# Loading and turning the first pair's q and k: strips of 128 bytes and VectorE transposes, or whole rows and fp32 products

## The chip, the cores and the metric

The kernel runs on one core of a Trainium2 chip. The metric is the device time of one execution in microseconds (us). Three runs of the kernel before took 267.16, 268.35 and 268.5 us, median 268.35; the run of 267.16 us is the profiled one. Its span, from the first to the last instruction, is 265.2 us, so 1.96 us lie around the span.

## The reference, cut to what matters

Attention over chunks of keys, followed by a mixture-of-experts layer with one expert per token. For each query the 24 chunks of 32 keys are ranked by an upper bound on their scores, made from the minimum and maximum of the chunk's keys in each dimension; only the best 6 chunks take part in the softmax.

```python
B, H, S, D = 4, 8, 768, 64          # attention; chunk = 32, top_k = 6
k_min, k_max = np.min(k_chunks, axis=3), np.max(k_chunks, axis=3)
ub = np.sum(np.maximum(q * k_min, q * k_max), axis=-1)   # broadcast over query x chunk
ub = np.where(causal, ub, -1e9)
top_chunks = np.argsort(ub, axis=-1)[..., -top_k:]
scores = np.where(sel & causal_by_token, (q @ k.T) / 8, -1e9)
attn = softmax(scores) @ v
x = attn.transpose(0, 2, 1, 3).reshape(B * S, H * D)     # 3072 x 512
# then: argmax expert per token, at most 80 tokens kept per expert (those with the largest gate),
# out[token] = gate * (relu(x @ w1[e]) @ w2[e]),  8 experts, 512 -> 1024 -> 512
```

## The kernel before, in words

The 32 (batch, head) combinations are worked in 16 pairs of heads: pair i holds heads 2p and 2p+1 of batch b, one in partitions 0 to 63 and the other in 64 to 127 (partition = head dimension, free axis = 768 tokens). The code is written out by hand in the order of issue; each engine works through its own instructions in that order, and a helper (`op`) adds the semaphore waits that follow from the names of what is read and written. So the order on an engine is the order in the source.

For each pair, q and k are needed turned: `qT` and `kT`, 64 dimensions by 768 tokens for both heads. In the kernel before, `load` brings q and k with four DMAs each (L377): a DMA of group g takes head g // 2, half g % 2 of the 64 dimensions, in pieces of 32 fp32 numbers (128 bytes), 768 pieces per DMA, so placed that VectorE's transpose of 32 x 32 blocks (`take_q` L456, `take_k` L466) leaves the tokens in order. For the first pair SP issues the groups of head 0 and ScalarE's queue those of head 1, k before q, and the loads of pair 1 and of v follow on SP. Then VectorE takes the minimum (`kmm`, L468) and the maximum (`kmx`, L471) of each chunk and their difference (L473), and ScalarE makes `rq`, the positive part of q (`take_r`, L460): the bound of a chunk is q . min + relu(q) . (max - min).

`bounds` (L489) forms that in PSUM with 16 products: eight on `qT` with the minima, then eight on `rq` with the differences. `score_mm` (L584) follows: q k products for the first steps into the PSUM tiles `SC0`, `SC1` and half of `OB`. Meanwhile `bounds_out` on VectorE turns the bounds, takes the eight largest of each query (L503) and marks the chunks that are not selected (`uns`, L508). `unselT` turns these marks by products (L520) and ScalarE copies them out (`unsT`, L525); products with `ind` (L606), a constant that spreads a chunk over its 32 keys, add the mask to the scores. ScalarE takes the exponentials (`EXB`, L616), GpSimd and VectorE clear the diagonal and add up the sums, and `values` (L731) multiplies by v. From there the loop over the pairs runs, with the bounds of the next pair made while the current one is finished. A gather of the selected tokens and the experts' products follow at the end.

`ind` is made once: VectorE fills it, GpSimd cuts the steps into 32 partitions of each half (L423, L425), and two ScalarE copies (L428) double them into the other 32.

`warm(n, w)` (L1178) issues n products of the bf16 identity with w columns into `SC0`. Nothing reads them; they keep TensorE busy. In the kernel before 52 products of 152 columns stand ahead of everything else on TensorE, and the first pair is then taken with

```python
warm(52, 152)
take_k(0, 0)      # VectorE: transpose k, minimum
take_q(0)         # VectorE: transpose q
take_r(0)         # ScalarE: relu(q)
take_k(0, 1)      # VectorE: maximum, difference
bounds(0)
```

Of the kernel before, what the change touches and what calls it, by code (L numbers as in the profile page):

```python
# [4 lines left out]
ALU = mybir.AluOpType  # L5
ACTF = mybir.ActivationFunctionType
# [4 lines left out]
AX = mybir.AxisListType.X  # L11
# [3 lines left out]
CHUNK = 32  # L15
# [132 lines left out]
def bass_quest_chunk_select__then__topk_capacity_drop_kernel(  # L148
# [10 lines left out]
    B, H, S, D = q.shape  # L159
# [4 lines left out]
    NT = S // 128  # L164
    NCH = S // CHUNK
# [42 lines left out]
    with ExitStack() as pers:  # L208
# [8 lines left out]
        ident_f = al(pers, "ident_f", [128, 128])  # L217
        ident_bf = al(pers, "ident_bf", [128, 128], BF16)
# [4 lines left out]
        sy = Sync(nc)  # L223
        op = sy.op

        with nc.Block(no_gpsimd_drain=True) as blk:

            @blk.sync
            def _body(_unused):
                sp = nc.sync  # L230
                gp = nc.gpsimd
                ve = nc.vector
                ac = nc.scalar
                pe = nc.tensor


                SC = [al(pers, f"SC{i}", [128, 1024], F32, True) for i in range(2)]
                OB = al(pers, "OB", [128, 1024], F32, True)
# [5 lines left out]
                qn = [al(pers, "qn", [128, NT, 2, D]) for _ in range(NB)]  # L244
# [3 lines left out]
                qT = [al(pers, "qT", [128, S]) for _ in range(2)]  # L248
# [118 lines left out]
                def load(i, what="qkv", eng="sp", gs=range(4), hs=(0, 1)):  # L367
                    b, p, s = i // NPB, i % NPB, i % NB
                    base = (b * H + 2 * p) * S * D
                    for nm, src, dst in (("qn", q, qn), ("kn", k, kn), ("vn", v, vn)):  # L370
                        if nm[0] not in what:
                            continue
                        if nm != "vn":
                            for g in gs:
                                a = bass.AP(src.tensor, src.offset + base + (g // 2) * S * D + (g % 2) * 32, [[D, 32], [32 * D, NCH], [1, 32]])
                                o = bass.AP(dst[s], g * 32 * 2 * NT * D, [[2 * NT * D, 32], [32, NCH], [1, 32]])
                                op(eng, lambda: sy.queue[eng].dma_start(o, a), w=[f"{nm}{s}{g}"], dsem=f"d_{nm}{s}{g}")  # L377
                            continue
                        for h in hs:
                            a = bass.AP(src.tensor, src.offset + base + h * S * D, [[D, 128], [128 * D, NT], [1, D]])  # L380
                            o = dst[s][:, :, h, :]
                            op(eng, lambda: sy.queue[eng].dma_start(o, a), w=[f"{nm}{s}{h}"], dsem=f"d_{nm}{s}{h}")
# [38 lines left out]
                for h in range(2):  # L421
# [2 lines left out]
                                                      base=0, channel_multiplier=-CHUNK), r=["ind"], w=[f"ind{h}"])  # L424
                    op("gp", lambda: gp.affine_select(o, o, pattern=[[-1, S]], compare_op=ALU.is_ge, fill=0.0,  # L425
                                                      base=CHUNK - 1, channel_multiplier=CHUNK), r=[f"ind{h}"], w=[f"ind{h}"])
                for h in range(2):
                    op("act", lambda: ac.activation(ind[h * 64 + 32:h * 64 + 64, :], ind[0:32, :], ACTF.Copy), r=["ind", "ind0"], w=[f"ind{h + 2}"])  # L428
                WG = ["wg0", "wg1"]

                def wload(e, part, after=()):
# [22 lines left out]
                def take_q(i):  # L454
                    j, s = i % 2, i % NB
                    op("dve", lambda: ve.transpose(qT[j][:], qn[s][:].rearrange("p a b c -> p (a b c)")),  # L456
                       r=[f"qn{s}{g}" for g in range(4)], w=[f"qT{j}"])

                def take_r(i):
                    op("act", lambda: ac.activation(rq[:], qT[i % 2][:], ACTF.Relu), r=[f"qT{i % 2}"], w=["rq"])  # L460

                def take_k(i, part=None):
                    j, s = i % 2, i % NB
                    kv = bass.AP(kT[j], 0, [[S, 128], [CHUNK, NCH], [1, CHUNK]])
                    if part != 1:
                        op("dve", lambda: ve.transpose(kT[j][:], kn[s][:].rearrange("p a b c -> p (a b c)")),  # L466
                           r=[f"kn{s}{g}" for g in range(4)], w=[f"kT{j}"])
                        op("dve", lambda: ve.tensor_reduce(kmm[j][:, 0, 0:NCH], kv, AX, ALU.min), r=[f"kT{j}"], w=[f"kmm{j}"])  # L468
                    if part == 0:
                        return  # L470
                    op("dve", lambda: ve.tensor_reduce(kmx[:], kv, AX, ALU.max), r=[f"kT{j}"], w=["kmx"])  # L471
                    e, q = ("gp", gp) if i > 1 else ("dve", ve)
                    op(e, lambda: q.tensor_tensor(kmm[j][:, 1, 0:NCH], kmx[:], kmm[j][:, 0, 0:NCH], ALU.subtract),  # L473
                       r=[f"kmm{j}", "kmx", "ind0", "ind1"], w=[f"kmd{j}"])

                def stripes(t, off, row, lo, n):

# [697 lines left out]

                def warm(n, w):
                    for _ in range(n):
                        op("pe", lambda: pe.matmul(SC[0][:, 0:w], ident_bf[:], bass.AP(ident_bf, 0, [[128, 128], [0, 2], [1, w // 2]]), start=True, stop=True),  # L1178
                           r=["ident_bf"], w=["SC0"], inc=False)

                def keep_warm(n, o=SC[0], k="SC0"):
# [7 lines left out]
                        op("pe", lambda: pe.matmul(M0[pr, 0:65], ident_f[:, pr], ident_f[:, 0:65], start=True, stop=True),  # L1189
                           r=["ident_f"], w=["M0"], inc=False)  # L1190

                warm(52, 152)
                take_k(0, 0)
                take_q(0)
                take_r(0)
                take_k(0, 1)
                bounds(0)
                score_mm(0, 0)
                score_mm(0, 1)
# [369 lines left out]
```

## Time and profile before

| | |
|---|---|
| median of 3 runs | 268.35 us (267.16 to 268.5) |
| profiled execution, its own time | 267.16 us |
| its span | 265.2 us |
| TensorE products (PE) | 253.8 us busy, 96% of the span |
| VectorE (DVE) | 211.3 us, 80% |
| GpSimd (POOL) | 206.5 us, 78% |
| ScalarE (ACT) | 160.9 us, 61% |
| DMA | 48.38 MB, 148619 packets, 131583 of them under 512 bytes |

The busy share of TensorE counts the `warm` products, which compute nothing. What sets the end is read from the chain that the profiler follows back from the last instruction; in the first 9 us this chain does not run over TensorE, though that engine is shown busy for most of them.

### The profile page before, as it was taken

To read this page: it belongs to the slowest core of one execution; us is meant where nothing else is said; L and a number is where in the kernel's file an instruction comes from. 1 tells how busy PE (TensorE), PEld (TensorE's weight loads), DVE (VectorE), ACT (ScalarE), POOL (GpSimd) and SP (SyncE) were. 2 spreads that over 40 slices of the span, in tenths; PEclk is the share of its full clock that TensorE was granted. 3 is DMA by queue.
4 is the path that set the end of the run, shared out by engine and by line. 5 is a ranking of instruction groups with operands and counts; after the bars stand their busy time and mean duration, and the time that the engine had idled before them with its cause. 6 is when DMAs were issued, how large, how long until landed. Compare 5 with 4: busy or idle time off the path is not lost.

```text
span 265.2 us, 9859 instructions
## 1 busy us (share of the span) xinstructions
PE 253.8 (96%) x4160; PEld 167.2 (63%) x4160; DVE 211.3 (80%) x592; ACT 160.9 (61%) x260; POOL 206.5 (78%) x288
## 2 busy tenths in 40 slices
PE   7799999999999999999999999999999999888993
PEld 7367576767666666666665656666556557665662
DVE  6887687687989988859899889899999988953342
ACT  3386757575787665656785656565865676841220
POOL 5168869895999798979998989988999942725842
PEclk9999999999999999999999999999999999999999
DMA  9989998999999989999999999969999982912771
GB/s 147 179 142 167 140 308 179 296 214 221 166 209 196 221 131 211 193 220 138 201 207 217 171 161 189 213 123 298 292 241 213 231 189 23 188 45 48 155 149 65
DMA packets 148619, 48.38 MB, mean 182 GB/s; under 512 B 131583, under 2 KB 138870, under 8 KB 148512
## 3 DMA queue, kind: packets, MB, share of 16 engines
q1 hardware_dynamic: 113552, 23.23, 44.9%
q0 software_dynamic: 9936, 18.64, 37.8%
q10 hardware_dynamic: 25088, 5.90, 11.3%
q8 instruction: 32, 0.52, 0.8%
q14 instruction: 11, 0.09, 0.1%
HBM read 57.03 MB, written 11.01 MB: 257 GB/s over the span
## 4 chain that ended last, share of the span: by engine, by line
PE 87%; DMA 4%; ACT 4%; DVE 2%; issue 1%; ACTq 1%; POOL 0%; DVEq 0%
PE OB L731 27%; PE SC L584 19%; PE SC L572 7%; PE SC L606 6%; PE MM L489 4%; PE OB L1499 4%; PE SC L1473 4%; PE MM L772 4%; PE MM L744 3%; DMA qn<-x_rows,idx 3%; PE OB L820 2%; DMA qn<-in_q_dram 2%; ACT EXB L616 1%; PE OB L572 1%; PE MM L811 1%; PE MM L529 1%
## 5 line engine op out<-in xcount | busy, mean ns | idle before, releaser
L616 ACT ACTIVATE EXB<-SC 128x1024 f32<-128x1024 f32 (+2 forms) x87 | 81.2, 947 | 33.3 <-PE SC L584 16.3
L684 POOL TENSOR_TENSOR ES<-ES,EXB 128x512 f32<-128x512 f32 (+1 forms) x73 | 77.6, 1066 | 4.9
L731 PE MATMUL OB<-EXB,vn 128*64 128x256 f32 (+2 forms) x640 | 69.3, 364 | 0.0
L584 PE MATMUL SC<-qT,kT 64*128 64x256 f32 (+3 forms) x376 | 60.8, 435 | 0.3
L731 PEld LDWEIGHTS OB<-EXB,vn 128*64 128x64 f32 x640 | 42.2, 137 | 21.0 <-issue 8.3
L684 POOL TENSOR_TENSOR ES<-EXB 128x512 f32<-128x512 f32 (+1 forms) x29 | 45.3, 1563 | 1.8
L584 PEld LDWEIGHTS SC<-qT,kT 64*128 64x128 f32 x376 | 31.1, 187 | 12.1 <-issue 7.7
L606 PE MATMUL SC<-unsT,ind 64*128 64x320 bf16 (+9 forms) x286 | 34.9, 303 | 0.1
L668 POOL TENSOR_SCALAR_AFFINE_SELECT EXB<-EXB 128x256 f32<-128x256 f32 x63 | 28.9, 465 | 5.0 <-ACT EXB L616 5.0
L739 ACT ACTIVATE oT<-OB 128x512 f32<-128x512 f32 (+1 forms) x32 | 15.7, 490 | 24.4 <-PE OB L731 24.4
L668 POOL TENSOR_SCALAR_AFFINE_SELECT ES<-EXB 128x256 f32<-128x256 f32 x15 | 6.3, 419 | 20.5 <-PE MM L772 13.7
L572 PE MATMUL SC<-qT,kT 64*64 64x256 f32 (+5 forms) x256 | 21.7, 436 | 0.0
L606 PEld LDWEIGHTS SC<-unsT,ind 64*128 64x128 bf16 (+1 forms) x286 | 12.3, 100 | 14.1 <-issue 7.4
L456 DVE STREAM_TRANSPOSE qT<-qn 128x768 f32<-128x768 f32 x16 | 15.5, 971 | 5.4 <-PE SC L606 4.9
L460 ACT ACTIVATE rq<-qT 128x768 f32<-128x768 f32 x16 | 13.5, 845 | 6.0 <-DVE qT L456 5.7
L534 ACT ACTIVATE unsT<-MM,cb 128x384 bf16<-128x384 bf16 (+1 forms) x30 | 14.2, 525 | 4.2 <-PE MM L529 4.0
L466 DVE STREAM_TRANSPOSE kT<-kn 128x768 f32<-128x768 f32 x16 | 15.5, 968 | 1.0 <-DMA kn<-in_k_dram 1.0
L468 DVE TENSOR_REDUCE kmm<-kT 128x24 f32<-128x768 f32 x16 | 15.3, 953 | 0.5
L471 DVE TENSOR_REDUCE kmx<-kT 128x24 f32<-128x768 f32 x16 | 15.1, 941 | 0.0
L503 DVE MAX8 top<-MM 128x8 f32<-128x8 f32 (+4 forms) x160 | 14.6, 166 | 0.6
L753 DVE STREAM_TRANSPOSE MM<-MM 128x192 f32<-128x192 f32 x16 | 6.3, 393 | 9.5 <-PE MM L772 9.2
L847 DVE TENSOR_TENSOR xp<-OB,rden 128x768 bf16<-128x768 f32 x14 | 13.4, 954 | 0.4
(274 smaller groups left out, 456.5 us busy)
## 6 DMA issues: line engine op xcount, KB each, us to landing
w1s<-in_moe_w_dram POOLq DMA_DIRECT2D x8, 1024.0 KB, 10.3
w2s<-in_moe_w_dram POOLq DMA_DIRECT2D x7, 1024.0 KB, 14.9
kn<-in_k_dram SPq DMA_DIRECT2D x62, 96.0 KB, 3.7
qn<-in_q_dram SPq DMA_DIRECT2D x62, 96.0 KB, 3.9
vn<-in_v_dram ACTq DMA_DIRECT2D x28, 192.0 KB, 5.7
out_dram<-w1s SPq DMA_DIRECT2D x2, 1536.0 KB, 6.7
out_dram<-out_dram SPq DMA_DIRECT2D x2, 1536.0 KB, 9.4
x_rows<-xp SPq DMA_DIRECT2D x7, 384.0 KB, 4.6
```

The costliest lines, as they stand in the source:

```text
L456: op("dve", lambda: ve.transpose(qT[j][:], qn[s][:].rearrange("p a b c -> p (a b c)")), r=[f"qn{s}{g}" for g in range(4)], w=[f"qT{j}"])
L466: op("dve", lambda: ve.transpose(kT[j][:], kn[s][:].rearrange("p a b c -> p (a b c)")), r=[f"kn{s}{g}" for g in range(4)], w=[f"kT{j}"])
L468: op("dve", lambda: ve.tensor_reduce(kmm[j][:, 0, 0:NCH], kv, AX, ALU.min), r=[f"kT{j}"], w=[f"kmm{j}"])
L471: op("dve", lambda: ve.tensor_reduce(kmx[:], kv, AX, ALU.max), r=[f"kT{j}"], w=["kmx"])
L572: op("pe", lambda: pe.matmul(o, kT[j][pr, k0:k0 + 64], qT[j][pr, q0 + cut:q1], start=not flags, stop=bool(flags)), r=[f"kT{j}", f"qT{j}"], ...
L584: op("pe", lambda: pe.matmul(o, kT[j][pr, ts(kt)], qT[j][pr, x0:x1], start=not flags and (not cols or cols[0] == 0) and n == 0, stop=bool( ...
L606: op("pe", lambda: pe.matmul(ps[ot, h * 512 + c0 + x:h * 512 + c1], ind[pr, k0:k0 + (64 if halves else 128)], unsT[j][pr, b0 - 128 + x:q1 ...
L616: op("act", lambda: ac.activation(Ex(st, None, 0, W, turned(i)), src, ACTF.Exp, scale=SCALE), r=pk, w=[f"E{st}"])
L668: op("gp", lambda: gp.affine_select(ad, a, pattern=[[0, 2], [1, 128]], compare_op=ALU.is_ge, fill=0.0, base=0, channel_multiplier=-1), r=[ ...
L684: op(e, lambda: sy.queue[e].tensor_tensor(o, in0, in1, ALU.add), r=[f"E{s2}", f"E{first[0]}"] if first else [f"E{s2}"] + (["E5"] if (s2, c ...
L731: op("pe", lambda: pe.matmul(OB[pr, q0:q1], vs[:, kt - RT, h, :] if kt >= RT and turned(i) else vn[s][:, kt, h, :], ex, start=(n == 0), st ...
L739: op("act", lambda: ac.activation(oT[:, q0:q1], OB[:, q0:q1], ACTF.Copy), r=[f"O{bk}"], w=[f"oT{bk}"])
```

## The change

For the first pair alone (i == 0) q and k are loaded in whole rows. A head comes with two DMAs: in the first each of the 128 partitions receives four consecutive tokens (1024 bytes), 512 tokens in all, in the second two consecutive tokens (512 bytes), the other 256. Both queues issue as many DMAs as before, in the same order.

The two VectorE transposes of this pair are gone. `turn_first` turns by products: one of six tiles of 64 dimensions by 128 tokens is the stationary operand and the fp32 identity the moving one, 6 tiles x 2 heads for k into `OB` and as many for q into `SC1`. The tokens of a tile are 4 (or 2) apart, so a product writes every fourth (or second) fp32 number of the PSUM row, and together the products leave the tokens in order. Minimum and maximum are taken from PSUM; ScalarE copies `qT`, `rq` and, last, `kT` out of PSUM. The two copies of `ind` move behind these three on ScalarE. The `warm` products become 6 of 456 columns ahead of the k products, 1 of 152 between k and q, and 4 of 456 behind q. The difference for pair 0 no longer waits for `ind`; for pair 1 it still names it.

```diff
--- before.py
+++ after.py
@@ -372,6 +372,12 @@
                             continue
                         if nm != "vn":
                             for g in gs:
+                                if i == 0:
+                                    n, t0 = (4, 0) if g % 2 == 0 else (2, 4)
+                                    a = bass.AP(src.tensor, src.offset + base + g // 2 * S * D + t0 * 128 * D, [[n * D, 128], [1, n * D]])
+                                    o = bass.AP(dst[s], g // 2 * NT * D + t0 * D, [[2 * NT * D, 128], [1, n * D]])
+                                    op(eng, lambda: sy.queue[eng].dma_start(o, a), w=[f"{nm}{s}{g}"], dsem=f"d_{nm}{s}{g}")
+                                    continue
                                 a = bass.AP(src.tensor, src.offset + base + (g // 2) * S * D + (g % 2) * 32, [[D, 32], [32 * D, NCH], [1, 32]])
                                 o = bass.AP(dst[s], g * 32 * 2 * NT * D, [[2 * NT * D, 32], [32, NCH], [1, 32]])
                                 op(eng, lambda: sy.queue[eng].dma_start(o, a), w=[f"{nm}{s}{g}"], dsem=f"d_{nm}{s}{g}")
@@ -424,8 +430,6 @@
                                                       base=0, channel_multiplier=-CHUNK), r=["ind"], w=[f"ind{h}"])
                     op("gp", lambda: gp.affine_select(o, o, pattern=[[-1, S]], compare_op=ALU.is_ge, fill=0.0,
                                                       base=CHUNK - 1, channel_multiplier=CHUNK), r=[f"ind{h}"], w=[f"ind{h}"])
-                for h in range(2):
-                    op("act", lambda: ac.activation(ind[h * 64 + 32:h * 64 + 64, :], ind[0:32, :], ACTF.Copy), r=["ind", "ind0"], w=[f"ind{h + 2}"])
                 WG = ["wg0", "wg1"]
 
                 def wload(e, part, after=()):
@@ -471,7 +475,7 @@
                     op("dve", lambda: ve.tensor_reduce(kmx[:], kv, AX, ALU.max), r=[f"kT{j}"], w=["kmx"])
                     e, q = ("gp", gp) if i > 1 else ("dve", ve)
                     op(e, lambda: q.tensor_tensor(kmm[j][:, 1, 0:NCH], kmx[:], kmm[j][:, 0, 0:NCH], ALU.subtract),
-                       r=[f"kmm{j}", "kmx", "ind0", "ind1"], w=[f"kmd{j}"])
+                       r=[f"kmm{j}", "kmx"] + (["ind0", "ind1"] if i else []), w=[f"kmd{j}"])
 
                 def stripes(t, off, row, lo, n):
 
@@ -1175,7 +1179,7 @@
 
                 def warm(n, w):
                     for _ in range(n):
-                        op("pe", lambda: pe.matmul(SC[0][:, 0:w], ident_bf[:], bass.AP(ident_bf, 0, [[128, 128], [0, 2], [1, w // 2]]), start=True, stop=True),
+                        op("pe", lambda: pe.matmul(SC[0][:, 0:w], ident_bf[:], bass.AP(ident_bf, 0, [[128, 128], [0, 4], [1, w // 4]]), start=True, stop=True),
                            r=["ident_bf"], w=["SC0"], inc=False)
 
                 def keep_warm(n, o=SC[0], k="SC0"):
@@ -1189,11 +1193,29 @@
                         op("pe", lambda: pe.matmul(M0[pr, 0:65], ident_f[:, pr], ident_f[:, 0:65], start=True, stop=True),
                            r=["ident_f"], w=["M0"], inc=False)
 
-                warm(52, 152)
-                take_k(0, 0)
-                take_q(0)
-                take_r(0)
-                take_k(0, 1)
+                def turn_first(n, ps, keys):
+                    for t in range(NT):
+                        lo, w = (t, 4) if t < 4 else (512 + t - 4, 2)
+                        for h in range(2):
+                            src = bass.AP(n, h * NT * D + t * D, [[2 * NT * D, 128], [1, D]])
+                            op("pe", lambda: pe.matmul(bass.AP(ps, h * 64 * 1024 + lo, [[1024, 64], [w, 128]]), src, ident_f[:], start=True, stop=True),
+                               r=[f"{'k' if n is kn[0] else 'q'}n0{2 * h + (t > 3)}", "ident_f"], w=keys, inc=(t == NT - 1 and h == 1))
+
+                kf = OB[:, 0:S].rearrange("p (c k) -> p c k", k=CHUNK)
+                warm(6, 456)
+                turn_first(kn[0], OB, ["O0", "O1"])
+                op("dve", lambda: ve.tensor_reduce(kmm[0][:, 0, 0:NCH], kf, AX, ALU.min), r=["O0", "O1", "kmm0"], w=["kmm0"])
+                warm(1, 152)
+                turn_first(qn[0], SC[1], ["SC1"])
+                op("act", lambda: ac.activation(qT[0][:], SC[1][:, 0:S], ACTF.Copy), r=["SC1"], w=["qT0"])
+                op("act", lambda: ac.activation(rq[:], SC[1][:, 0:S], ACTF.Relu), r=["SC1"], w=["rq"])
+                op("dve", lambda: ve.tensor_reduce(kmx[:], kf, AX, ALU.max), r=["O0", "O1"], w=["kmx"])
+                op("dve", lambda: ve.tensor_tensor(kmm[0][:, 1, 0:NCH], kmx[:], kmm[0][:, 0, 0:NCH], ALU.subtract),
+                   r=["kmm0", "kmx", "kmd0"], w=["kmd0"])
+                op("act", lambda: ac.activation(kT[0][:], OB[:, 0:S], ACTF.Copy), r=["O0", "O1", "kmx"], w=["kT0"])
+                warm(4, 456)
+                for h in range(2):
+                    op("act", lambda: ac.activation(ind[h * 64 + 32:h * 64 + 64, :], ind[0:32, :], ACTF.Copy), r=["ind", "ind0"], w=[f"ind{h + 2}"])
                 bounds(0)
                 score_mm(0, 0)
                 score_mm(0, 1)
```

Where the instructions stand, engine by engine (a row is a line of the kernel, the operation, what it writes and reads, the size, and the semaphores it waits for; `sy_dve` is VectorE's, `sy_act` ScalarE's, `sy_pe` TensorE's, `sy_gp` GpSimd's, `sy_d_kn00` that of a DMA into `kn`). TensorE before, from the last of the 52 `warm` products to the first scores:

```order
L1178 MATMUL SC_18<-ident_bf 128x152 x51
L489 MATMUL MM<-qT,kmm 32x160 [waits sy_dve]
L489 MATMUL MM<-qT,kmm 32x160 x7
L489 MATMUL MM<-rq,kmm 32x160 [waits sy_act]
L489 MATMUL MM<-rq,kmm 32x160 x7
L584 MATMUL SC_18<-qT,kT 128x512 x2
```

TensorE now, from the turn of q (the turn of k stands ahead of it in the same form, with its own four waits for the loads) to the first scores:

```order
L1201 MATMUL SC_19<-ident_f,qn 64x128 [waits sy_d_qn00]
L1201 MATMUL SC_19<-ident_f,qn 64x128 [waits sy_d_qn02]
L1201 MATMUL SC_19<-ident_f,qn 64x128 x6
L1201 MATMUL SC_19<-ident_f,qn 64x128 [waits sy_d_qn01]
L1201 MATMUL SC_19<-ident_f,qn 64x128 [waits sy_d_qn03]
L1201 MATMUL SC_19<-ident_f,qn 64x128 x2
L1182 MATMUL SC_18<-ident_bf 128x456 x4
L493 MATMUL MM<-qT,kmm 32x160 [waits sy_dve,sy_act]
L493 MATMUL MM<-qT,kmm 32x160 x7
L493 MATMUL MM<-rq,kmm 32x160 [waits sy_act]
L493 MATMUL MM<-rq,kmm 32x160 x7
L588 MATMUL SC_18<-qT,kT 128x512 [waits sy_act]
```

TensorE now waits for the loads itself, and the first score product has a wait for ScalarE that it did not have. ScalarE before, from the table load to the copy of the marks:

```order
L394 ACTIVATE dmy<-dmy 128x1 [waits sy_dve]
L428 ACTIVATE ind<-ind 32x768 [waits sy_gp]
L428 ACTIVATE ind<-ind 32x768
L460 ACTIVATE rq<-qT 128x768 [waits sy_dve]
L525 ACTIVATE unsT<-MM 128x2x3x64 [waits sy_pe]
```

ScalarE now:

```order
L400 ACTIVATE dmy<-dmy 128x1 [waits sy_dve]
L1210 ACTIVATE qT<-SC_19 128x768 [waits sy_pe]
L1211 ACTIVATE rq<-SC_19 128x768
L1215 ACTIVATE kT<-OB 128x768 [waits sy_dve]
L1218 ACTIVATE ind<-ind 32x768 [waits sy_gp]
L1218 ACTIVATE ind<-ind 32x768
L529 ACTIVATE unsT<-MM 128x2x3x64 [waits sy_pe]
```

Two copies of 768 columns are new, and `ind` stands behind all three. VectorE before, from its last preparing instruction to the turn of the bounds:

```order
L420 MEMSET ind 128x768
L466 STREAM_TRANSPOSE kT<-kn 128x768 [waits sy_d_kn02,sy_d_kn03,sy_d_kn01,sy_d_kn00]
L468 TENSOR_REDUCE kmm<-kT 128x24 [waits sy_dve]
L456 STREAM_TRANSPOSE qT<-qn 128x768 [waits sy_d_qn02,sy_d_qn03,sy_d_qn01,sy_d_qn00]
L471 TENSOR_REDUCE kmx<-kT 128x24
L473 TENSOR_TENSOR kmm<-kmx,kmm 128x24 [waits sy_gp,sy_dve]
L496 STREAM_TRANSPOSE MM<-MM 128x160 [waits sy_pe] x2
```

VectorE now:

```order
L426 MEMSET ind 128x768
L1207 TENSOR_REDUCE kmm<-OB 128x24 [waits sy_pe]
L1212 TENSOR_REDUCE kmx<-OB 128x24
L1213 TENSOR_TENSOR kmm<-kmx,kmm 128x24 [waits sy_dve]
L500 STREAM_TRANSPOSE MM<-MM 128x160 [waits sy_pe] x2
```

The two transposes are gone, and the first reduction waits for TensorE in place of the DMAs.

## Rows read from the trace of the kernel before

**Rows 1.** Page, part 4: shares of the span on the chain that ended last.

```profile
PE 87%; DMA 4%; ACT 4%; DVE 2%; issue 1%; ACTq 1%; POOL 0%; DVEq 0%
```

**Rows 2.** Chain of waits, from the start to 23 us: start us, us, what.

```profile
2.50 4.10 DMA qn<-in_q_dram
...
6.78 0.89 DVE qT L456
...
7.67 0.92 DVE kmx L471
...
8.62 0.20 DVE kmm L473
...
8.86 0.78 PE MM L489 x32
9.63 1.92 PE SC L584 x8
11.55 0.43 PE OB L584 x4
...
12.01 0.34 PE MM L520 x10
...
12.37 0.50 ACT unsT L525
...
13.29 3.78 ACT EXB L616 x4
...
17.12 0.49 PE SC L584 x4
...
17.66 0.70 PE MM L489 x32
18.37 4.69 PE OB L731 x48
```

**Rows 3.** Timeline, first 13 us: start us, us, engine, line, operation [idle before <-releaser].

```profile
1.83 5.22 PE L1178 MATMUL SC<-ident_bf 128*128 128x152 bf16 x52 [1.83 <-DVE kmm L400]
...
4.90 0.98 DVE L466 STREAM_TRANSPOSE kT<-kn 128x768 f32<-128x768 f32 x1 [0.84 <-DMA kn<-in_k_dram]
...
5.87 1.71 ACT L428 ACTIVATE ind<-ind 32x768 bf16<-32x768 bf16 x2 [1.29 <-POOL ind L425]
5.91 0.95 DVE L468 TENSOR_REDUCE kmm<-kT 128x24 f32<-128x768 f32 x1
...
9.15 0.48 PE L489 MATMUL MM<-rq,kmm 64*32 64x160 f32 x16
...
9.72 0.60 DVE L496 STREAM_TRANSPOSE MM<-MM 128x160 f32<-128x160 f32 x2 [0.92 <-PE MM L489]
...
11.54 0.41 DVE L508 TENSOR_TENSOR uns<-MM,top 128x240 bf16<-128x240 f32 x1
```

**Rows 4.** DMA traffic in 2.0 to 6.4 us: packets, bytes, mean rate.

```profile
DMA packets 7257, 0.91 MB, mean 207 GB/s; under 512 B 7257, under 2 KB 7257, under 8 KB 7257
```

**Rows 5.** DMA rate in 40 slices of 10 to 14 us, rows of 256 bytes.

```profile
GB/s 159 146 138 151 198 172 341 210 233 251 246 248 231 220 215 243 253 274 271 251 259 279 279 284 277 233 156 100 59 38 36 21 18 18 33 97 166 243 279 284
```

**Rows 6.** Windows of line L1178: stretch, then busy us (instructions); PEclk is the granted clock.

```profile
core 0: us, PE busy (x) PEld busy (x), PEclk, DMA share, GB/s
2.00:4.00 2.00, 2.00 (x18) 2.00 (x17) 1.00 1.25 198
5.60:6.60 1.00, 1.00 (x19) 1.00 (x17) 1.00 1.38 215
```

**Rows 7.** Groups by line and shape: line, engine, tiles, shapes, count | busy us, mean ns.

```profile
L616 ACT ACTIVATE EXB<-SC 128x768 f32<-128x768 f32 x8 | 6.5, 816 | 0.0
...
L847 DVE TENSOR_TENSOR xp<-OB,rden 128x768 bf16<-128x768 f32 x14 | 13.4, 954 | 0.4
```

**Rows 8.** Timeline of ScalarE (ACT) from 16.9 us.

```profile
16.93 0.87 ACT L460 ACTIVATE rq<-qT 128x768 f32<-128x768 f32 x1
17.66 1.32 ACT L616 ACTIVATE EXB<-SC 128x1024 f32<-128x1024 f32 x2
```

## The prediction

> **What bounds the kernel now.** I read the page's chain by shares first, then the chain in order of time over the first 23 us, then the timeline of the same stretch. The shares say that TensorE carries 87% of the span and DMA 4% [rows 1]; the change touches only the first pair, so the question is where that chain is not yet TensorE. In order of time it starts with the loads: q lands at 2.50 + 4.10 = 6.60 us, VectorE transposes q (6.78), takes the maximum (7.67) and the difference (8.62), and the bounds start at 8.86 [rows 2]. k had landed just ahead of 4.90, where VectorE's first transpose ends a wait of 0.84 us for it [rows 3]. TensorE is shown busy from 1.83 to 7.05, but with the 52 products that nobody reads [rows 3]. So up to 8.86 two things are level: q's landing and VectorE's five instructions.
>
> The bounds end at 9.63, and then two ways run side by side to 12.01: on TensorE the scores (1.92 + 0.43 us, to 11.98), on VectorE the search for the eight largest, which ends at 11.54 + 0.41 = 11.95 [rows 2, 3]. Both must be done before the marks are turned at 12.01, since that product stands behind the scores on TensorE. Then ScalarE copies the marks at 12.37 and takes four exponentials without a gap, 13.29 to 17.07; from 17.12 TensorE goes on to the bounds of pair 1 and into the products with v [rows 2]. From here there is little slack to swallow a shift, so I let what is gained or lost at 12.01 go to the end in full.
>
> **The change part by part.** The terms are times at which each step ends.
>
> Loads: q and k together are 2 x 2 x 768 x 64 x 4 = 786 KB. Before, packets of 128 bytes (0.91 MB in 7257 packets) moved at 207 GB/s [rows 4]. From 2.0 us, k's half takes 1.9 us to 3.9 and landed some 0.95 later; both take 3.8 us to 5.8 and landed 0.8 later. For rows of 512 and 1024 bytes there is no row. One bound is 207 GB/s, nothing gained: k at 4.87, q at 6.60. The nearest other row is 284 GB/s, the best slice of v's loads in rows of 256 bytes [rows 5]. I take it: k at 2.0 + 1.4 + 0.95 = 4.3, q at 2.0 + 2.8 + 0.8 = 5.6. Still faster rows would help k little: the six `warm` products ahead of it last until 4.08 (below).
>
> TensorE's pace: 16 of the 152-column products go by in 2 us up to 4 us, 0.125 us each, and 16 in one us from 5.6 on, 0.0625 each [rows 6] (17 are counted, one cut by the edge). That is 1.2 and 2.4 GHz; the granted clock reads 1.00 in both rows, so that column doesn't show it. 52 products in 5.22 us at these two paces put the rise near 5.4 us, after unbroken work from 1.83. Six products of 456 columns at the lower pace take 6 x 3 x 0.125 = 2.25 us, to 4.08.
>
> Turn of k and q: 12 products each. The products with v have the same shape, 128 rows by 64 columns of weights in fp32, and go in pairs, one head in each half: 24 products, 5,376 columns, in 4.69 us [rows 2], 0.223 us for a pair of 128 columns; half the clock makes 0.447. k starts at 4.33: 2.4 pairs until 5.4, the other 3.6 in 0.80, end 6.20. The filler (152 columns) ends at 6.26. q is there since 5.6: six pairs, 1.34 us, end 7.60.
>
> A price that only a page states: "PSUM — Partial Sum Buffer" of the Trainium skill, section Specifications, says that PSUM has lines of 8 bytes and that any access pattern that isn't contiguous slows products significantly. The turned rows are written every 16 or 8 bytes. No run here shows a product that writes in such steps; by that rule the turn would be a rival (below).
>
> VectorE: the two transposes go. Minimum and maximum of 768 columns take 0.95 us from SBUF [rows 3]; for PSUM the nearest row is another operation on 768 columns of it, 0.954 [rows 7]. So 6.28 to 7.23, 8.18, and with the difference (0.20 on the chain, rows 2) 8.4.
>
> ScalarE: three passes over 768 columns from PSUM, 0.82 to 0.87 us each [rows 7, 8], but the next one starts 0.73 after the one before [rows 8]. Between the end of a product and the start of its reader lie 0.09 us (9.63 to 9.72, rows 2, 3); from ScalarE's end to TensorE 0.05 (17.07 to 17.12, rows 2). qT 7.69 to 8.52, rq 8.42 to 9.25, kT 9.15 to 9.98. So qT comes after the difference, and the first eight bounds start at 8.57. The second eight need rq: 9.30, plus 0.48 as before [rows 3], end 9.78. That is 0.15 later than 9.63. The first score product waits for kT, the last of the three: 10.03 in place of 9.63, **0.40 later**. The scores take 2.35 us as before and end at 12.38; the marks are ready at 11.95 + 0.15 = 12.10 and wait. So the wait for q and VectorE's queue at the start becomes a wait for ScalarE's, and the turn of the marks moves by +0.4 us.
>
> Edits that I cost at nothing: the four `warm` products behind q (4 x 3 x 0.0625 = 0.75, to 8.35) fit ahead of 8.57; at the lower clock they would last to 9.1 and the second eight bounds would end some 0.1 later, still under the scores. The two copies of `ind`, 1.71 us [rows 3], start at 9.88 and end at 11.6, with a copy of the marks due behind them at 12.7; without that 1.1 us of cover they would delay it one for one. Dropping the wait of the difference for `ind` gains nothing: VectorE is later there. The DMAs are as many on the same queues. Pair 2's load of q now waits for TensorE's turn, but 14 DMAs of pair 1, v and the gate stand ahead of it on SP. VectorE's two freed slots (some 1.9 us) lie in front of a wait for the bounds (0.92 us, rows 3) and buy nothing.
>
> Sum: the profiled execution took 267.16 us; with +0.4 it is 267.6. It was the fastest of three; from the median of 268.35 the forecast is **268.7 us**. A measurement of this kernel can tell about 0.5% from no change, 1.34 us; this is within it.
>
> **Rivals.**
> *Rows land no sooner.* k at 4.87, 1.1 pairs until 5.4, 4.9 x 0.223, end 6.49; q from 6.63 to 7.97. That is 0.37 later than 7.60: +0.8, 269.1. For it: nothing here shows longer rows at work on these queues. Against: 256 bytes already did better than 128.
> *The clock is up earlier.* If it rises ahead of k's products, k ends at 5.67 and q at 7.07, 0.53 sooner: -0.1; if the rows land early as well (k at 4.1), q ends at 6.84 and it is -0.4: 268.0 to 268.2. kT still comes last, 2.4 us behind q's end, which is why even this gains little.
> *Steps in PSUM halve the products' pace.* Place: the 12 pairs of the turn. If only the part at full clock suffers, k takes 2.4 pairs until 5.4 and 3.6 x 0.447, end 7.0, and q 2.68, end 9.74: 2.14 later, +2.5. If the lower pace halves too, 1.2 pairs, then 4.8 x 0.447, end 7.55, q at 10.3: +3.1. So 270.9 to 271.4, slower. It makes the kernel slower than can be missed (+1.34, so 0.94 beyond the forecast) from a mean of 0.35 us per pair, where I have 3.2 us for 12, 0.27. For it: every other product in the rows writes its columns side by side, so none speaks. Against: an fp32 product takes four times as long per column as a bf16 one (0.223 us for 128 columns against 0.0625 for 152), so writes may have room. By the PSUM page's rule it would be this case.
> *The clock stays low through the turn.* k ends at 7.01, q at 9.82: +2.6, 270.95; if it rises in between, q at 8.41, +1.2, 269.6. Against: TensorE works with a gap of some 0.25 us at 4.1 where before it had none.
>
> **How the numbers follow.** Forecast 0.55; rows no sooner 0.10; clock up earlier 0.15; steps in PSUM 0.13; clock low 0.04; something late in the program, as the gathers, that shifts with the start, 0.03. None of the cases gains 1.34 us; the scatter of the runs before (1.34 us between the ends of three) leaves 0.05 for faster. Slower is the PSUM case, half of the low clock and the rest of the scatter: 0.13 + 0.02 + 0.03 = 0.18. Same 0.77. The range goes from 267.1 (the lowest case less 0.9 of scatter) to 270.9, the lower end of the PSUM case; the likeliest case alone would be 267.9 to 269.5.
>
> **What would show it.** Right: the products of the turn end near 6.2 and 7.6; the bounds start before 8.86 and their second half pauses for rq; the first score product waits for ScalarE's kT, near 10.0; the marks are turned near 12.4 with VectorE done before. The landing is right if TensorE starts k's products near 4.3. Wrong: a pair at 0.4 us or more at full clock (PSUM steps), q's products waiting for a DMA, or the score products starting ahead of 9.63. If the marks are turned later and the end doesn't move, the shift was swallowed, and my step from 12.01 to the end is wrong.

## The result, and the profile after

The changed kernel takes 269.31 us, median of 13 runs (268.01 to 271.28), against 267.53 us, median of 13 runs of the kernel before beside them (266.82 to 270.88): a ratio of 1.0066 with an interval of 1.0049 to 1.0083, so 1.3 to 2.2 us slower. The measured time lies 0.6 us above the forecast of 268.7 us and inside the range; but the loss of 1.78 us is past the 1.34 us, 0.5%, that I had called no change. The profiled execution is the one of 269.31 us; its span is 267.4 us. Medians here and below are over all runs; the ratios and their intervals leave out the slow runs, two of the kernel before beside e1 to e4 and one of e2.

The chain of waits of the changed kernel, in order of time (start, duration, what; the trace counts an fp32 product twice, so x24 are 12 products, six pairs):

```profile
1.83 2.46 PE SC L1182 x6
4.29 2.76 PE OB L1201 x24
7.05 0.24 PE SC L1182
7.29 1.84 PE SC L1201 x24
9.16 0.81 ACT qT L1210
9.97 0.70 ACT rq L1211
10.67 0.71 ACT kT L1215
11.43 1.99 PE SC L588 x8
14.95 3.78 ACT EXB L620 x4
20.03 4.69 PE OB L735 x48
221.48 2.54 PE MM L815 x126
264.17 0.97 POOL out_dram L1527
```

The last two of these in the kernel before:

```profile
219.81 2.53 PE MM L811 x126
262.02 0.97 POOL out_dram L1505
```

Against [rows 2], q's landing and VectorE's instructions are gone from the chain, as they should be. In their place stand 12 pairs of products (L1201) and three ScalarE passes. The exponentials start at 14.95 in place of 13.29, the products with v at 20.03 in place of 18.37: 1.66 us later, and that shift is still whole at 221.48 (219.81 before, 1.67). What takes the room is the turn: k lasts 2.76 us where I had 1.87, and q ends at 9.1, not 7.60.

The products of the turn in windows of 0.4 us (columns: window; busy and count of products, of weight loads; granted clock; DMA share; GB/s):

```profile
4.80:5.20 0.40, 0.40 (x8) 0.40 (x6) 1.00 1.19 280
5.60:6.00 0.40, 0.40 (x8) 0.40 (x6) 1.00 1.37 202
7.60:8.00 0.40, 0.40 (x8) 0.40 (x6) 1.00 1.09 174
8.00:8.40 0.40, 0.40 (x12) 0.40 (x9) 1.00 0.72 118
```

The count goes from 8 to 12 only at 8.0 us (a window's edges cut some products, so it doesn't double). So the clock rose from 1.2 to 2.4 GHz there, and not near 5.4 as in the execution of [rows 6]. As in [rows 6], the granted clock reads 1.00 on both sides.

The DMAs of k's last rows and of q's first and last rows, all on ScalarE's queue, in the changed kernel (size, us from issue to landing):

```profile
kn<-in_k_dram ACTq DMA_DIRECT2D x1, 64.0 KB, 2.8
qn<-in_q_dram ACTq DMA_DIRECT2D x1, 128.0 KB, 4.4
qn<-in_q_dram ACTq DMA_DIRECT2D x1, 64.0 KB, 4.8
```

They were issued at 1.3, 1.75 and 2.2 us, so they land at 4.1, 6.1 and 7.0 us. In [rows 2] q had landed at 6.60: rows bring k sooner, but not the end of q.

VectorE and the turn of the marks in the timeline of the changed kernel (start, duration, engine, line, operation; in brackets the idle time before it and what ended it):

```profile
7.10 0.96 DVE L1207 TENSOR_REDUCE kmm<-OB 128x24 f32<-128x768 f32 x1 [3.04 <-PE OB L1201]
7.97 0.95 DVE L1212 TENSOR_REDUCE kmx<-OB 128x24 f32<-128x768 f32 x1
13.13 0.41 DVE L512 TENSOR_TENSOR uns<-MM,top 128x240 bf16<-128x240 f32 x1
13.68 0.31 PE L524 MATMUL MM<-ident_bf,uns 64*128 64x64 bf16 x10
```

The extremes cost from PSUM what they cost from SBUF [rows 3]. The marks are turned at 13.68, 1.67 later than 12.01.

### The profile page after: what moved, and what is told of

Same layout as the page of the kernel before. It is cut to its first block, busy times and chain, and to the rows that moved or that the text cites. A ratio compares the mean times of both kernels' runs of the same rounds, so it can differ in the third digit from the quotient of the medians.

```text
span 267.4 us, 9870 instructions
## 1 busy us (share of the span) xinstructions
PE 257.1 (96%) x4167; PEld 167.4 (63%) x4167; DVE 209.4 (78%) x590; ACT 162.2 (61%) x262; POOL 206.7 (77%) x288
## 4 chain that ended last, share of the span: by engine, by line
PE 89%; ACT 5%; DMA 2%; DVE 2%; issue 1%; POOL 0%; ACTq 0%; DVEq 0%; POOLq 0%
PE OB L735 26%; PE SC L588 18%; PE SC L576 7%; PE SC L610 6%; PE OB L1521 4%; PE SC L1495 4%; PE MM L493 4%; PE MM L776 4%; PE MM L748 3%; DMA qn<-x_rows,idx 2%; PE OB L824 2%; ACT EXB L620 2%; PE OB L1201 1%; PE OB L576 1%; PE SC L1182 1%; PE MM L815 1%
## 5 line engine op out<-in xcount | busy, mean ns | idle before, releaser
L460 DVE STREAM_TRANSPOSE qT<-qn 128x768 f32<-128x768 f32 x15 | 14.6, 970 | 5.0 <-PE SC L610 5.0
L464 ACT ACTIVATE rq<-qT 128x768 f32<-128x768 f32 x15 | 12.7, 845 | 5.2 <-DVE qT L460 4.7
L472 DVE TENSOR_REDUCE kmm<-kT 128x24 f32<-128x768 f32 x15 | 14.3, 953 | 0.5
L470 DVE STREAM_TRANSPOSE kT<-kn 128x768 f32<-128x768 f32 x15 | 14.5, 967 | 0.1
L475 DVE TENSOR_REDUCE kmx<-kT 128x24 f32<-128x768 f32 x15 | 14.1, 943 | 0.0
```

## The experiments

Three theories stand against each other. A: the moment at which TensorE's clock rises differs from execution to execution, and the changed kernel hands it on to the end. B: the products ahead set that moment. C: the clock has no part in it; the steps in PSUM or ScalarE's passes make the loss.

**Same program again, and the work in front of it.** Three kernels, with one question: is 8.0 us a property of this program? The first is the changed kernel itself; the second has 18 products of 152 columns ahead of k's turn, the third eight of 456 columns on a constant that is ready sooner, from 1.13 us on.

```
e2:  -warm(6, 456)   +warm(18, 152)
e3:  -warm(6, 456)   +ve.memset(OHS[:, 0:128], 1.0)   # first on VectorE
                     +8 x pe.matmul(SC[0][:, 0:456], OHS[:, 0:128], OHS as 4 x 114 columns)
```

> The changed kernel once more, unchanged. Theory A (the moment at which TensorE goes from 1.2 to 2.4 GHz differs from execution to execution, and the turn by products now shows it in the time): the rise is read from the pace of the turn's products and may lie anywhere from about 5 to 8.5 us, other than the 8.0 us of the first profile by 0.3 us or more; the marks are then turned at 12.0 + 0.4 to 12.0 + 2.2 us, and the runs scatter over 2 to 3 us. Theory B (the kind of products ahead sets the rise): the rise is at 8.0 us again within 0.2, the marks at 13.7, the runs within 1 us of each other. Both: +0.4 to +2.2 us against before.

> The changed kernel with 18 products of 152 columns ahead of the turn of k in place of 6 of 456, as many columns. Theory B, in the form that the wide products with few weight loads delay the rise: the rise comes near 5.4 us as in the kernel before, k's turn ends near 6.2 and the time falls by about 1.2 us against the changed kernel, to +0.4 of before. Theory A: the rise lies anywhere, and over the rounds the time is that of the changed kernel within its scatter (about +1.7 us of before, plus or minus 1).

> The changed kernel with 8 products of 456 columns ahead of the turn that read a tile set by VectorE's first instruction, so that TensorE starts near 1.1 us and not 1.83. Both theories let the rise move ahead by some 0.7 us on average, and the time with it by 0.4 to 0.8 us, to about +1.0 of before; k's products still start near 4.2. If the clock had nothing to do with the loss (rival C: the turned rows written in steps, or ScalarE's three passes, make the whole of it), the time stays at +1.7.

Measured, with before at 267.5: 268.21 us (ratio 1.0043, interval 1.0001 to 1.0085), 269.37 (1.0057, 1.0017 to 1.0097) and 268.32 (1.0027, 0.9994 to 1.006). The first one's timeline, the same program as above:

```profile
4.22 1.81 PE L1201 MATMUL OB<-ident_f,kn 128*64 128x128 f32 x24
6.14 1.53 PE L1201 MATMUL SC<-ident_f,qn 128*64 128x128 f32 x24
9.98 1.99 PE L588 MATMUL SC<-qT,kT 64*128 64x512 f32 x8 [0.20 <-ACT kT L1215]
12.24 0.31 PE L524 MATMUL MM<-ident_bf,uns 64*128 64x64 bf16 x10
```

Here k takes 1.81 us, the clock is up from 5.0, q ends at 7.67 and the marks are turned 0.23 after 12.01. One program, 1.44 us apart at the marks by the moment of the rise alone: q's products end 1.44 us apart (7.67 and 9.11), and the rest is the same. Behind the same six products the rise came at 8.0 and at 5.0, so B in its plain form falls here; what is left of it is that unbroken 152-column products, as in the kernel before, set the moment at 5.4. In e2 it lies near 5.2, in e3 near 6.0 though TensorE starts 0.7 us sooner (marks at 12.37 and 12.74). The intervals of the three overlap, so they rank nothing.

**Transposes in place of products.** Six fp32 transposes of 128 x 128 per tensor, both heads at once, with pieces of 256 bytes in the loads so that the heads lie side by side:

```
-for h in range(2): pe.matmul(..., src of head h (64 columns), ident_f[:], ...)
+pe.transpose(bass.AP(ps, lo, [[1024, 128], [w, 128]]), src of both heads, ident_f[:])
```

> The changed kernel with the turn made by 6 fp32 transposes of 128 by 128 per tensor in place of 12 products, both heads in one, and for that the heads laid side by side, so that the loads write pieces of 256 bytes. The trace of before has such transposes, 272 ns each and half as many instructions per tile as a product; at half the cost the turn of k and q takes 1.3 us each at 1.2 GHz and 0.65 at 2.4, where the first profile has 2.76 and 1.84. Theories A and B: k's turn ends near 5.6, q's then waits for the load of q (near 6.5 to 7.0) and ends at 7.2 to 8.0, the marks are turned near 12.0 to 12.6, the time is -0.2 to +0.6 of before and scatters less than the changed kernel. Rival C (writing in steps or ScalarE): no better than the changed kernel less 0.3.

Measured 270.01 us, ratio 1.0074 (1.0036 to 1.0111). The turn does get cheaper, but q now waits for its DMA, in two pieces (k's last two transposes wait for theirs too, to 5.39):

```profile
4.16 1.68 PE L1200 MATMUL OB<-ident_f,kn 128*128 128x128 f32 x6
6.39 0.66 PE L1200 MATMUL SC<-ident_f,qn 128*128 128x128 f32 x4 [0.49 <-DMA qn<-in_q_dram]
7.38 0.44 PE L1200 MATMUL SC<-ident_f,qn 128*128 128x128 f32 x2 [0.34 <-DMA qn<-in_q_dram]
```

The edit changes two things at once: with pieces of 256 bytes q's last rows land at 7.3 and not at 6.5 to 7.0, so it doesn't price the transposes alone. The marks come at 12.38, so 0.4 us is lost there; the rest is lost 220 us later, and the time is outside what A and B gave (up to 0.6 us over before). The time alone is what C gave, but what is lost that late is not lost in the turn. Behind the gather of rows the products of L1053 run at half clock in this execution:

```profile
234.00:236.00 2.00, 1.80 (x16) 1.53 (x13) 0.50 0.45 98
236.00:238.00 2.00, 1.54 (x11) 1.08 (x8) 0.65 0.00 0
```

The granted clock reads 0.50 and 0.65 there, and 1.00 in the same windows of the profiled executions of before and after. Nine of this kernel's ten runs have a mean clock of 0.994 or less. That is a second source of scatter; a third profile of the kernel before (below) has it too. Why it hits this kernel so often stays open.

**Steps in PSUM, no warming, a split pass, and before again.** e5 writes the turned columns side by side (the first pair's tokens are then out of order, the work is the same), e6 is the kernel before, e7 leaves out the products ahead of k, e8 gives half of `rq` to VectorE.

```
e5:  -lo, w = (t, 4) if t < 4 else (512 + t - 4, 2)    +lo, w = t * 128, 1
e7:  -warm(6, 456)
e8:  -ac.activation(rq[:], SC[1][:, 0:S], Relu)        +ac.activation(rq[:, 0:384], ...)
                                                       +ve.tensor_scalar(rq[:, 384:S], qT[0][:, 384:S], 0.0, None, ALU.max)
```

> The changed kernel, but each product of the turn writes its 128 columns side by side in PSUM instead of every 16 or 8 bytes; the tokens of pair 0 are then out of order, so the values of that pair differ, the work does not. Theory A (the pace of TensorE's clock, not the steps): a pair of products takes 0.46 us ahead of the rise and 0.24 to 0.25 us behind it, as with the steps (2.76 us for six, 1.49 us for six); q's six pairs take 1.49 us if the clock is up by then, 1.8 if it rises in between. Theory C (steps in PSUM cost): six pairs at the upper pace take 1.34 us (0.223 each, the pace of the products with v), and six at the lower one 2.68.

> The kernel before, unchanged, for a second look at its start. Theory A (the moment at which the clock rises differs between executions, and the kernel before hides it): the pace of the 152-column products changes from 0.125 to 0.0625 us at another moment than 5.4 us, anywhere from 4.6 to 8.3; they end between 6.3 and 8.33 (52 at the lower pace), still ahead of the bounds, which start at 8.8 to 8.95 whatever the rise. Theory B (the kind of products sets the moment): 5.3 to 5.5 again. Time 266.7 to 268.5 by both.

> The changed kernel without the six products ahead of k's turn, so that TensorE does nothing before k lands. Theory A (the loss is the time that the turn spends at 1.2 GHz, handed on to the end): k's six pairs 4.25 to 7.0, all at 0.46 us; q's from 7.05, ending 9.8 if the clock stays low or 8.5 to 9.2 if it rises in between; marks turned at 13.4 to 14.7, 1.4 to 2.7 us later than the 12.01 of before, and the time 268.9 to 270.3 with before at 267.5 (ratio 1.005 to 1.010). Theory C (the loss is ScalarE's three passes and the steps, whatever the clock): the end of the products does not carry over, and the time stays at the 268.2 to 269.3 of the changed kernel, ratio 1.003 to 1.0065, with the marks within 0.4 us of those of the changed kernel at the same ratio.

> The changed kernel, with the second half of rq (columns 384 to 767) taken by VectorE from qT in SBUF behind the difference, so that ScalarE's third pass, kT, comes some 0.35 us sooner. With the clock up near 5 us as in the repeat run: qT 7.72 to 8.53, half of rq on ScalarE to 8.95 and on VectorE 8.6 to 9.1, second half of the bounds 9.15 to 9.63, kT to 9.7, scores from 9.7 in place of 9.98, marks at 12.05 to 12.1 in place of 12.40. Theory A: the time falls by that 0.3 us and no more, 267.9 to 269.0 by the moment of the rise; with the clock late (8.0) the marks come at 13.3 or so. Theory C (ScalarE's queue makes the loss of 1.78 us): most of the loss goes, 267.5 to 267.9.

e5 took 269.42 us in its one run. Its chain:

```profile
4.29 2.76 PE OB L1201 x24
7.23 1.49 PE SC L1201 x24
```

Six pairs take 2.76 us at the lower clock and 1.49 at the upper with the columns side by side; with steps of 16 and 8 bytes they take the same 2.76 (above) and, in the chain of e1, the same 1.49:

```profile
6.21 1.49 PE SC L1201 x24
```

The steps cost these products nothing. In e5 the rise fell between k and q, near 7.1.

The kernel before (e6) took 267.88 us, with the rise near 5.4 as in the first profile, bounds at 8.86 and marks at 12.01:

```profile
1.83 5.26 PE L1178 MATMUL SC<-ident_bf 128*128 128x152 bf16 x52 [1.83 <-DVE kmm L400]
```

What was left of theory B stood after that; e12, below, decides.

e7 took 268.85 us (ratio 1.0039, 1.0009 to 1.007), just under the edge of what theory A gave it, and inside what C gave; so it is the marks that decide. Its timeline:

```profile
3.71 2.90 PE L1201 MATMUL OB<-ident_f,kn 128*64 128x128 f32 x24 [3.71 <-DMA kn<-in_k_dram]
6.78 2.83 PE L1201 MATMUL SC<-ident_f,qn 128*64 128x128 f32 x24
14.18 0.31 PE L524 MATMUL MM<-ident_bf,uns 64*128 64x64 bf16 x10
```

All 12 pairs at the lower clock, and marks at 14.18, 2.17 late: the dose that theory A asks for, handed on in full to the products with v (20.53, 2.16 late). But its ten spans reach from 265.9 to 268.7 us; on the median the six products ahead of k buy nothing that this measurement sees.

e8 took 268.46 us (ratio 1.0032, 1.0016 to 1.0047):

```profile
7.22 1.80 PE L1201 MATMUL SC<-ident_f,qn 128*64 128x128 f32 x24
13.28 0.32 PE L524 MATMUL MM<-ident_bf,uns 64*128 64x64 bf16 x10
```

From the end of q's products (9.02) to the marks it is 4.26 us, against 4.57 in e7 (9.61 to 14.18), in e1 (7.67 to 12.24), and within 0.01 in the changed kernel, e2, e3 and e5. So half of ScalarE's pass is worth 0.31 us, as expected, and with the rise near 7.9 the marks are still 1.27 late and the time is above the 267.5 to 267.9 of theory C. Theory C, which gives the clock no part, falls: but for e8, the same 4.57 us follow on q's products in all of them, and the end of q's products moves with the clock.

**Which theory holds for the rise.** e9 puts 33 of the old products ahead of k; e10 changes q alone, with k as before and 39 old products ahead of q; e11 and e12 are the changed kernel and the kernel before, unchanged, each for a third profile.

```
e9:  -warm(6, 456)   +warm(33, 152)
e10: load: rows for "qn" only;  warm(39, 152); take_k(0, 0); turn_first(qn[0], SC[1]);
     qT and rq by ScalarE; take_k(0, 1); warm(4, 456); the copies of ind in their old place
```

> The changed kernel with 33 products of 152 columns in front of k's turn in place of six of 456, the same products as in the kernel before, so that with a rise near 5.4 us as in both looks at it k's turn starts at 5.7, behind the rise. Theory B (the products ahead set the moment: behind unbroken 152-column ones the clock rises at 5.4, while with fp32 products ahead it came at 5.0, 7.1, 7.6 and 8.0): k 5.7 to 7.2, q 7.3 to 8.8, all at 0.25 us for a pair; scores 11.1, marks 13.5, that is 1.5 us later than before; time 268.8 to 269.2 with before at 267.3. Theory A (the moment moves between executions whatever is ahead): another moment than 5.3 to 5.5 in the profile, and with one of 7 or later the filler lasts to 5.95, k ends at 8.2 or later and the marks come at 14 or later, 269.4 or more.

> One part alone: q in rows of 1024 and 512 bytes and turned by products, copied and taken through Relu by ScalarE; k as in the kernel before (blocks of 128-byte pieces, VectorE's transpose, extremes from SBUF), the copies of ind in their old place, and 39 products of 152 columns ahead of q. ScalarE has no third pass and only six pairs of products meet the clock. With a rise at 5.4 us the 39 end at 6.1; q turned 6.2 to 7.7 if it has landed, qT 7.8 to 8.6, rq to 9.3, second half of the bounds 9.35 to 9.83, scores from 9.83, marks at 12.15 to 12.2: 0.15 to 0.2 us later than 12.01. Theory A or B (the loss is turning at 1.2 GHz, the rest ScalarE's third pass): 267.5 to 267.8 with before at 267.3. Theory C (products and PSUM passes cost by themselves): half the loss of the changed kernel, 268.1 or more, at marks near 12.2.

> The changed kernel, unchanged, for a third look at the moment of the rise (8.0 us in the first, 5.0 in the second; 7.1 and 7.6 in two kernels whose TensorE work up to there is the same). Theory A: any moment between 4.6 and 9.6; the marks come 2.35 to 2.45 us behind the end of kT's copy, which ends 3.1 us or so behind q's last product, so their turn lies at 12.4 for a rise by 5.0 and up to 14.4 for one that comes behind q. Theory B: 7 to 8 again, since fp32 products stand ahead, marks at 13.3 to 13.9.

> The kernel before, for a third look (5.4 us in both others). Theory B: 5.3 to 5.5. Theory A: any moment between 4.6 and 8.3. In both the bounds start at 8.86 and the marks are turned at 12.01, since the 52 products end ahead of 8.4 at either pace.

The kernel before ran 2.3 us faster beside these four, 264.98 us. e11 took 267.21 and e12 266.62 in their one run. The kernel before, windows of its 152-column products in e12:

```profile
5.00:6.00 1.00, 1.00 (x11) 1.00 (x9) 1.00 1.38 215
6.00:7.00 1.00, 1.00 (x11) 1.00 (x10) 1.00 1.37 213
7.00:8.00 1.00, 1.00 (x13) 0.89 (x11) 1.00 0.85 136
```

The count is 11 until 7 us, where [rows 6] has 19 from 5.6 on: the clock rose near 7.5. The same execution's timeline:

```profile
1.83 6.26 PE L1178 MATMUL SC<-ident_bf 128*128 128x152 bf16 x52 [1.83 <-DVE kmm L400]
8.85 0.51 PE L489 MATMUL MM<-qT,kmm 64*32 64x160 f32 x16 [0.76 <-DVE kmm L473]
12.00 0.32 PE L520 MATMUL MM<-ident_bf,uns 64*128 64x64 bf16 x10
```

The products last a microsecond longer than in [rows 3] and end at 8.09, the bounds start at 8.85 and the marks are turned at 12.00. Theory B is refuted, and the cover is seen: the kernel before has the same wandering rise, and it costs nothing, because behind the products TensorE waits for VectorE anyway. Later in the same execution the clock falls, as in e4:

```profile
232.00:234.00 2.00, 1.60 (x15) 1.39 (x16) 0.67 0.04 9
234.00:236.00 2.00, 1.74 (x12) 1.23 (x10) 0.50 0.46 91
```

The changed kernel in e11, a third moment for the one program:

```profile
4.22 2.66 PE L1201 MATMUL OB<-ident_f,kn 128*64 128x128 f32 x24
6.99 1.53 PE L1201 MATMUL SC<-ident_f,qn 128*64 128x128 f32 x24
13.08 0.31 PE L524 MATMUL MM<-ident_bf,uns 64*128 64x64 bf16 x10
```

The rise lies near 6.7, the marks 1.07 late. Another 0.6 us is lost on the way to 220 us: the loss grows between 69 and 83 us, where ScalarE stands 0.84 us at 72.90 for no wait that the profile shows. e9 took 267.93 us (four runs, ratio 1.0115, 1.006 to 1.017): the rise came at 5.8 in the profile, outside the 5.3 to 5.5 that theory B gave, all 12 products of each turn ran at the upper clock, and the marks came at 13.67:

```profile
5.94 1.53 PE L1201 MATMUL OB<-ident_f,kn 128*64 128x128 f32 x24
13.67 0.31 PE L524 MATMUL MM<-ident_bf,uns 64*128 64x64 bf16 x10
```

At the marks, waiting for the clock costs as much as turning without it did in the first profile. The marks are 1.66 of the 2.95 us between the medians; with four runs the rest isn't settled. e10 took 266.52 us (1.006, 1.0022 to 1.0097). In its profile the clock rose at 5.3 and things went as both theories had it:

```profile
6.09 1.53 PE L1203 MATMUL SC<-ident_f,qn 128*64 128x128 f32 x24
12.12 0.32 PE L526 MATMUL MM<-ident_bf,uns 64*128 64x64 bf16 x10
```

Marks 0.11 late. But the median is 1.5 us over before, where A gave 0.2 to 0.5: a miss, for I had priced one moment only. Its time is what C gave (0.8 or more, at marks near 12.2). At the lower clock to the end, the 39 products would last to 1.83 + 39 x 0.125 = 6.7, and q 2.76 more, to 9.46: by this estimate 1.84 later than here. The profiled execution itself, 266.7 us with an early rise, also loses about 0.6 between 83 and 98 us, near a pause of TensorE of 0.37 us that I can't explain, and takes 28.9 us from its experts' first products to the end, where e11 takes 27.6. So this median is not settled by the rise, and a cost of q's new path that doesn't show at the marks isn't excluded.

## Why the prediction was right or wrong

**Landing: near for k, wrong for q.** k's last rows land at 4.1, with 4.3 forecast. The sign that I gave for it, TensorE's start on k near 4.3, could not tell: the start at 4.22 is set by the products ahead, and in e7, without them, it comes at 3.71. q was put at 5.6; its last rows land at 7.0 in the profiled execution and at 6.5 in e1, against 6.60 before. "Rows land no sooner" was a rival, and for q it came true. It cost nothing only because the first four tiles of q's turn need just the first rows (6.1, and 5.9 in e1, where the turn starts at 6.14), and these are there when k's turn ends; the last two tiles come up later than the last rows. In the windows above the DMA rate is 280 GB/s near 5.0 and 202 near 5.8; the 128-byte loads of pair 1, issued from 2.69 on, move then too, but whether they hold q back was not tried.

**The clock's rise: the step that failed.** "52 products in 5.22 us at these two paces put the rise near 5.4 us" was read from one execution and used as a constant. (As a sum the two paces give 5.8; the starts of the products in the trace, 0.127 us apart and then 0.066, do give 5.4, since the last product takes 0.23 us to end.) Three profiles of the kernel before gave 5.4, 5.4 and 7.5; three of the changed one 8.0, 5.0 and 6.7. "The clock stays low through the turn" had a chance of 0.04 and prices of +1.2 to +2.6; the profiled execution, with +1.67, lies between these. The argument against it, that TensorE pauses only 0.25 us, was none: the moment also moves where there is no pause.

That the forecast of 268.7 lies only 0.6 us from the measurement is luck: it adds 0.4 us to 268.35, the median of three runs, where 13 runs gave 267.53; the shift was 1.78 us and not 0.4.

The spans show the spread without a profile. Beside e7, 13 of 19 spans of the kernel before lie between 265.2 and 265.5 us; the 13 of the changed one are spread from 266.0 to 268.9. Five executions whose TensorE work is the same up to the turn (the changed kernel three times, e5, e8) have their marks 0.23, 1.07, 1.25, 1.27 and 1.67 us late, 1.10 on the mean (e8's would be 0.31 later without its split pass). The measured loss is 1.3 to 2.2 us in the first comparison and 0.0 to 2.3 in e1's. Of the 1.78 us between the medians of the first, the marks explain some 1.1 to 1.7; the rest is not settled (below: behind 221 us, and outside the span).

**The turn's pace: right, but for its end.** Six pairs take 1.49 us at the upper clock and 2.76 at the lower, 0.248 and 0.46 for a pair, where I had 0.223 and 0.447. Within a turn the pairs start 0.22 us apart (q in e10) and 0.43 (q in e7), as I had them; what I left out is some 0.2 us in each turn until its last product has ended. With the rise at 5.0 q ends at 7.67, which I had for a rise at 5.4 at 7.60.

**From q to the marks: a little high.** Forecast 7.60 to 12.41, 4.81 us; measured 4.57. ScalarE's chain was right in its structure, and the scores do wait for kT: in e1, where the rise is near the forecast's, qT starts at 7.72 (7.69 forecast), the bounds at 8.58 (8.57) and the scores at 9.98 (10.03). The marks follow the first scores by 2.26 us (9.98 to 12.24) and not by 2.38.

**Steps in PSUM: rightly a rival, refuted.** e5 decides: the columns side by side change nothing. "PSUM — Partial Sum Buffer" of the Trainium skill, section Specifications, would have steps slow the products significantly; for these fp32 products the measurement says no (2.76 and 1.49 us either way).

**From 12.01 to the end in full: right up to 220 us.** The shift is still whole at 221.48. Of the eleven profiled executions with the new turn, nine reach this line as late as their marks, within 0.16 us; e10 and e11 lose 0.4 and 0.6 on the way. Of the last stretch I can say less: the profiled execution starts its last piece at 264.17, 2.15 after the 262.02 of before, so about 0.5 us more is lost behind 221 us, in a part that the change doesn't touch.

**Same at 0.77: too high.** The loss is 1.78 us, with an interval of 1.3 to 2.2, and the bound was 1.34. With the rise anywhere between 5.0 and 8.0 the cases run from +0.2 to +1.7, up to and past that bound and not well inside it, and no moment makes the kernel faster: the marks stay at 12.01 only if q ends by 7.44, and e1, with the earliest rise seen, ended it at 7.67. No experiment beat the kernel before.

## What to carry to other kernels

Before moving work onto TensorE at the start of a program, ask what it costs at 1.2 GHz, and whether a wait that no engine can shorten lies behind it; a pace read from one execution there is a sample, not a constant. The same work on another engine, in front of a wait, may look slow and be worth keeping as cover. If most executions of a kernel agree to 0.3 us and those of the changed one spread over 2.9, take the spread for the finding and profile the same program two or three times before explaining the median.

## What the runs showed that I had not expected

- The moment of the rise is not set by the program: it came at 5.0, 6.7 and 8.0 us in one, and at 5.4, 5.4 and 7.5 in another. What sets it stays open; e7, where TensorE had done nothing before 3.71 us, had all 12 pairs of its turn at the lower pace, to 9.6.
- The clock can fall again behind the wait for the gather: granted clock 0.50 from 234 to 236 us in e4 and e12, 0.50 from 236 to 238 in e7. In e4 TensorE was busy for 0.35 of the 2 us before. Of the kernel before, 8 of 31, 3 of 19 and 2 of 13 runs have a mean clock of 0.994 or less, so it is no property of the change.
- The time outside the span is 1.9 to 2.0 us in the 63 runs of the kernel before that stood beside the experiments, but 2.5 to 4.2 in some of those of the changed kernel (3.0 and 4.2 in the first comparison, 3.3 and 3.6 in e1, 2.5 in e11), 2.1 to 3.4 in some of e2 and e3, and 3.0 in e5. It wasn't tried what this is.
- An fp32 transpose of 128 x 128 turns both heads in half the time of two products: in e4 the transposes start 0.11 us apart at the upper clock and 0.21 at the lower, the pairs of products 0.22 and 0.43. What is missing there is the data: both turns wait for their DMAs.
